# Queries and keys of three batches transposed by the DMA crossbar instead of TensorE, with a newly searched order of work

## The chip, the cores and the metric

The kernel runs on one core of a Trainium2 chip. The metric is the device time of one execution in microseconds (us). A single core has faster and slower executions too: one that is over 1.5% above the fastest of the same kernel is called slow, and ratios use fast runs alone.

A ratio below is the mean time of one kernel's fast runs over that of the kernel before in the same rounds, with a 95% interval. It is not quite the ratio of the medians that stand beside it. Where I turn a ratio into microseconds, I multiply its distance from 1 by 180 us.

## The reference

An attention over 4 batches, 8 heads, 768 positions and 64 dimensions feeds a gated long convolution. Each position sees 8 global keys and the last 96 positions.

```python
def _attn_ref(q, k, v, n_global, n_local):
    scores = scale * np.matmul(q, k.transpose(0, 1, 3, 2))
    # ... bias by distance, everything but global and local keys masked
    a = np.exp(scores - max)
    return np.matmul(a / sum, v)

def _moe_ref(x, w_proj, filter_fft, w_out):
    x1, x2, x3 = thirds of (x @ w_proj)
    x2_conv = irfft(rfft(x2) * rfft(filter_fft))
    return (x1 * x2_conv * x3) @ w_out
```

## The kernel before

The program is a graph of operations with costs. A list scheduler with searched weights (NUDGES) lays them out ahead of time, and each engine then runs its list in that fixed order. Loads of query, key and value rows are issued by GpSimd, stores and small copies by the SP queue.

Queries and keys arrive as rows and are needed with the head dimension on partitions. Batch 0 has its own path, which the change leaves alone. For batches 1 to 3, TensorE transposes four 128x128 blocks into a PSUM bank, and ScalarE or VectorE copies the bank out:

```python
self.qn = t("qn", [P, 6, H, D])      # rows, one buffer for all batches
self.kn = t("kn", [P, 7, H, D])
self.QT = t("QT", [P, 4, S])         # transposed, one buffer as well
self.KT = t("KT", [P, 4, 7 * P])

def transposes(self, what, t, src, cols):
    b = g.bank()
    def turn(_):
        for i in range(4):
            nc.tensor.transpose(b.f16()[:, P * i:P * i + P],
                                src[:, 2 * i:2 * i + 2, :], self.ident)
    g.op("P", pe(*[128] * 4), turn, acq=[b], ...)
    dst = ...                                    # a piece of QT or KT
    g.op("AV", ..., lambda e: self.copy(e, dst, b.f16()...), use=[b], ...)
    if what == "k" and t == 0:                   # the 8 global keys, to the front of each tile
        g.op("V", dve(224), lambda _: self.copy("V", kv[:, :, :, 0:NG], ...), ...)

def scores(self, hp, gi, near=False, pair=False):
    ...                                          # KT against QT, then exp on ScalarE
```

Because qn, kn, QT and KT exist once, they form a ring. A load of the next batch needs this batch's rows transposed, and a transpose needs the scores of the batch before to have read QT and KT.

The softmax here doesn't subtract the row's maximum and nothing guards it: scores larger than these inputs give would overflow.

Of the kernel before, what the change touches and what calls it, by code (L numbers as in the profile page):

```python
# [16 lines left out]
P = 128  # L17
NG = 8
# [21 lines left out]
BEGIN = 1.0  # L40
# [24 lines left out]
class Plan:  # L65
# [90 lines left out]
    def lay(self):  # L156
# [10 lines left out]
        out = []  # L167
        for o in self.ops:
            o.rank = o.batch[0] + o.batch[1] * o.tail / (total[o.batch] or 1.0) + o.bias + o.noise
        while live:  # L170
# [33 lines left out]
            if o.bytes:  # L204
                n, size = o.bytes
                cost = 0.007 + 3.6e-5 * size if e == "S" else 0.0045 + 3.7e-5 * size
                x = "SG".replace(e, "")
                at, work, each[e] = max(dma[e], o.end + 1.0), n * cost / 16, cost
                slow = 1.0 + each[x] / cost
                both = min(max(0.0, dma[x] - at), slow * work)  # L210
                dma[e] = at + both + work - both / slow
                ready = o.landed = dma[e] + 2.1
                if e == "G":
                    lanes.append(ready)
# [21 lines left out]
        -26671, 1454, -27060, 644, -34526, -2914, -25286, -6925, -45676, -4611, -20860, 1460, 2723, 7789,  # L236
        -8273, -9648, -2460, -18439, 5853, -13712, -13265, -5361, 9436, 3579, -30354, -6495, -3967, 2837,
        -13308, 7637, 1168, 7200, -12925, 8898, -12205, 12435, -32726, 4718, -4396, -6557, 7468, -1990,
        -3553, -11575, -8488, -6307, 8992, -12791, 23613, 4548, -30667, 7678, -2661, 40439, 23, 3822, 25223,
        19000, 9598, 7189, 9787, 23821, -11341, 23456, -11755, 5738, -6127, 39, 3279, 34899, -27473, 7686,  # L240
        5753, 21416, 6632, 26871, 8728, 6700, -3360, 18664, 10344, 10332, -16596, 12142, -10605, 14405,
        -25027, -150, 4813, -1741, 6716, 5345, -5698, 894, -21964, 8631, 14489, -201, 15618, 9598, 7510,
        4151, -7056, -21, 32636, 2899, -11225, -6462, 6929, -304, -21733, 21997, 9940, -5190, 9087, 636,
        -5187, -573, -12475, -4124, -8380, -671, -12776, 4813, -3686, 1361, -2133, 9833, -12744, 7014, 828,
        13335, 519, -7496, -1970, -5267, 3910, -7020, 8778, -5167, 3049, -39, 44238, -22392, 3868, -5492,
        5032, -11948, 883, -8512, 25357, -7798, 18676, -15531, 4417, -16339, 13865, -1852, 23684, -21598,
        13514, 17858, 17257, -557, 13373, 6339, 16373, -9272, -4058, -25687, 26062, 9023, 16287, -2105,
        6700, 2623, -3578, -5898, 15188, -9520, 15932, 4326, 21030, 6734, 2015, 1958, -25233, 9143, -34251,
        -13125, -16742, -592, -6891, -15887, -9801, -48606, -12178, 2086, -15877, -25133, -1600, 2379,
        -23801, -14531, 20195, 15173, 12449, 263, -17906, -3700, 14906, 1186, -19366, -14660, -2718, 3254,  # L250
        -20486, -7203, -4412, -15788, -38649, -6418, -1655, 10753, -17734, -21313, 32361, 393, 8516, -16517,
        21564, 1605, 17688, -3061, -10380, -4180, -14573, 4840, -13690, -17777, -9155, 18474, -7161, -29302,
        -313, -1665, -19374, -7420, -9795, 1024, -6732, 29494, 24754, -8266, -9187, -12630, 17723, 6915,
        -11585, 9057, -17244, -16606, 3040, -3366, 6885, -37386, 9683, -15183, -31661, -37889, -7819, 2466,
        -43791, -22140, 13121, -13710, 10401, 1807, 4765, 14336, -10814, -10169, 21045, -19960, 7933,
        -28620, 4211, -2811, 31233, 6868, -22348, 7890, -2864, -3743, 11427, -9576, 6080, -16630, 30799,
        1411, -4032, -3274, -9417, -2532, 9740, -10826, 28438, 5562, 26589, 793, -40417, 5892, -36342,
        -5644, 12849, -30590, 31141, 14444, -22328, -12896, -34168, -8150, -57913, -5204, 15711, 1235, 6293,
        2213, -6086, 8688, -22799, -4727, -21975, 17194, -3757, 10396, 28637, -4968, -17049, 3259, -12065,
        -270, -4906, -13608, 20080, -17815, 28876, 3572, -8777, -22175, -21175, 18592, 15224, -14329,  # L260
        -11261, -10500, -9164, -9393, 13199, -26402, -4645, -15202, -9299, -525, -6777, -7165, -9244, -9225,
        -12419, -15805, -7708, 2178, -7241, 5647, 21012, -4991, 6401, -2334, -5140, -15069, -20652, 5961,
        -35697, -3611, 3644, 12613, 47972, -1640, -2197, -11800, -5777, -7189, -2610, 3952, -203, 6913,
        15527, 7240, -16137, -6679, -3937, 834, -9611, 5105, 47, 4543, -11122, -4503, 13644, -16722, -24463,
        -17316, 12192, -10915, -20126, 1382, -8962, -10346, -24211, 12202, -33855, -21067, -21629, -2645,
        -5398, 11363, 4058, 2571, 6248, -2867, -3454, -7013, 8111, -4165, 25648, 9706, -4648, -11997, 8847,
        11920, -27944, -21197, 2222, -9255, -9101, -11207, -15647, 3068, 13863, -5612, 8378, 9103, -8882,
        -8677, -24972, -18852, -16277, -12182, 13199, -18976, -10170, 1364, 3773, 11230, 24038, 8526, 1626,
        15020, 3004, 30489, -4629, -331, 10528, 1419, 13574, 6549, 21821, 15228, 20766, 7684, 26770, 25798,
        -6498, -4789, -24449, -1245, -16178, 5655, -2810, 1595, 9574, 8409, 17611, 9924, -11306, 5323,  # L270
        12431, 4942, 33467, 24985, -10121, -311, -22495, 6019, -12210, 28768, -6886, -9465, 1431, 3236,
        14926, 8794, 2903, -275, -15940, 3474, 11924, 140, 18537, -2691, 3215, 4369, -7883, 10255, -2377,
        887, 1506, 8351, 2749, -2666, 1724, -2, -8763, -5759, 1279, 11205, -777, -15691, 3883, 5909, 4026,
        -9324, -6840, 3413, 6573, 10766, 6716, 11440, 1465, 3772, -14379, 1234, -13313, -5734, 7025, -2665,
        9733, -6834, 8271, 2042, 3032, -4621, 7425, -2600, 10085, -9127, 3381, -1345, 10211, -15378, 14859,
        6857, 8081, 211, -1467, -11827, -16185, 6723, -5950, -24265, -11782, -11476, -732, 5043, -7070,
        -927, -9965, 11218, -19986, 8589, -7968, 10143, 2808, 7080, -15962, 18025, -6488, -499, -21061,
        14160, 525, 514, -5066, -3068, 941, -12317, 489, 8578, 2311, -1959, -40040, 7983, 8312, 9946,
        -11449, 18822, -1699, 8498, 7623, 5090, -32147, 7079, 13071, 8675, -18625, 26688, 5401, 9760, -3054,
        -5688, 10887, 17782, -13291, 8915, -23867, 1484, -9206, 905, -50212, 11474, -9340, 12839, -13268,  # L280
        429, 3871, 17041, -25961, 10524, -8593, 29296, -26306, 6518, 14317, 1927, -27757, 14545, 15984,
        18775, -25044, -5453, 16461, 12339, -26421, 21502, 24783, 12969, -26891, 4376, 2513, 21873, 3194,
        -8112, -21024, 21259, -11197, 9391, -9675, -1356, 5710, -303, -16301, -11560, -30198, -10455, 6734,
        -10213, -20174, -19011, -27667, -4423, 4767, 13297, -32900, -12768, -27091, -7505, -2906, -20,
        34459, -2712, -3019, -702, -10293, -1211, 1634, 4234, -39114, -9749, 2253, 2533, 4712, 13540,
        -13115, -7066, 9629, 10055, 5131, 16930, -44240, -1286, 1203, 11673, -8416, 4726, -23705, 231,
        20816, 5391, -3140, 21876, 6812, 8588, -2283, 324, -40884, 10010, -9762, 8391, 14654, -15576, 1269,
        -1921, -1740, 998, -15686, -13359, -15492, -1021, 16161, -8349, -8154, 14786, -2046, 9528, -19999,
        1098, 10795, 12962, -13145, -12603, -1488, -5242, -44098, 21514, -2107, -9950, 17508, -780, -9857,
        6702, -3077, 14242, -28282, -6503, 2982, -12743, -9010, 2470, -6831, -13960, -21890, 6529, -21690,  # L290
        -992, -19558, -6249, -3225, 12323, -17611, -30223, 131, 4811, -10703, -2324, -2227, -11059, 5994,
        2855, -856, 5707, 21867, 785, 65, 15347, -11442, -3622, -17986, -7314, 12817, -2221, 2881, 9966,
        -2027, 698, 10775, -14082, -20635, 9561, -14262, 4552, -5388, 10443, -24604, -307, -2081, -2703,
# [89 lines left out]
        -8861, 21389, -11049, 17509, 41686, -10618, 9220, 25781, -14448, 18101, -8955, -3503, -7033, 43740,  # L383
        -10951, -8268, 11031, -2994, -4936,
    )
    FAVOUR = 0.1

    def fill(self, out):

# [75 lines left out]
class Fused:  # L465
# [173 lines left out]
    def load_v(self, b, ts):  # L639
# [4 lines left out]
        for t in ts:  # L644
            self.load_rows(("vn", s), vt, self.v, b, t)
            if t == 0:
                self.load_global(vt, s)
# [755 lines left out]
```

## Time and profile before

| | before |
|---|---|
| time, median (range) | 180.75 us (179.53 to 181.28, 4 runs of the comparison) |
| span of the profiled run | 179.1 us |
| TensorE busy | 170.3 us, 95% |
| VectorE busy | 161.0 us, 90% |
| ScalarE busy | 154.1 us, 86% |

The page below gives the DMA engines' busy share over 40 equal slices of the span (4.5 us each, 9 is 90% or more), the hardware queue (packets, MB, share of the time of 16 engines), and the row loads with their median time from issue to landing, the last number.

```profile
DMA  5999999999999999999990000000260000023344
...
q1 hardware_dynamic: 5920, 9.63, 15.1%
...
kn<-in_k_dram POOLq DMA_DIRECT2D x21, 120.0 KB, 6.2
qn<-in_q_dram POOLq DMA_DIRECT2D x18, 128.0 KB, 6.3
```

While loads run, up to about 93 us, the DMA row stands at 9 without a break. A digit adds up the time of all packets in the slice over 16 engines, and packets overlap: the queue of the row loads (q0, software_dynamic) alone has 107.1% of the span. So a 9 says that there are transfers in flight all the time, and no digit can show more.

### The profile page before, as it was taken

What the parts mean: (1) busy time and instruction counts of PE and PEld (TensorE: products, weight loads), DVE (VectorE), ACT (ScalarE), POOL (GpSimd) and SP (SyncE); (2) the same over time, 40 slices, a digit from 0 to 9 for tenths busy, and PEclk for the clock granted to TensorE, in tenths of its full rate; (3) what the DMA queues carried; (4) which work ended last, traced back from release to release, by engine and by line L of the source; (5) the groups of instructions that cost most, each with busy time, mean ns of one, the idle gap of its engine ahead of it and who ended that gap; (6) DMA issues with size and microseconds to landing.
All of it is one profiled execution on the core that took longest, in us unless ns stands there. A gap on an engine that the chain in (4) does not pass through costs nothing.

```text
span 179.1 us, 4509 instructions
## 1 busy us (share of the span) xinstructions
PE 170.3 (95%) x1732; PEld 105.3 (59%) x1732; DVE 161.0 (90%) x380; ACT 154.1 (86%) x311; POOL 70.0 (39%) x90
## 2 busy tenths in 40 slices
PE   7998799999999999999999999999999999999990
PEld 2456487566445657966456658854564784456540
DVE  6779679999999899999996998999999999999950
ACT  8699599987999999999869899999859997978751
POOL 7973692994988998998400000000000000000000
PEclk9999789999999999999999999999999999999997
DMA  5999999999999999999990000000260000023344
GB/s 184 334 251 112 167 207 166 149 177 140 182 150 140 120 146 114 129 158 139 170 298 21 0 4 0 4 0 0 103 243 10 4 2 0 4 115 119 117 176 178
DMA packets 79573, 21.19 MB, mean 118 GB/s; under 512 B 70424, under 2 KB 76480, under 8 KB 79552
## 3 DMA queue, kind: packets, MB, share of 16 engines
q0 software_dynamic: 73632, 11.28, 107.1%
q1 hardware_dynamic: 5920, 9.63, 15.1%
q8 instruction: 13, 0.21, 0.6%
q14 instruction: 8, 0.07, 0.1%
HBM read 25.69 MB, written 6.29 MB: 179 GB/s over the span
## 4 chain that ended last, share of the span: by engine, by line
PE 73%; DVE 8%; DMA 6%; POOL 4%; ACT 4%; issue 2%; POOLq 0%; ACTq 0%
PE bank L1085 22%; PE bank L1194 12%; PE bank L1146 9%; DMA vn<-in_v_dram 6%; PE bank L911 6%; PE bank L962 4%; PE bank L1168 4%; PE bank L925 4%; PE bank L1047 4%; PE bank L1002 4%; PE bank L1007 3%; POOL vn L575 2%; ACT E L977 2%; DVE E L984 1%; PE bank L1171 1%
## 5 line engine op out<-in xcount | busy, mean ns | idle before, releaser
L1085 PE MATMUL bank<-xT,w 128*128 128x384 f16 x256 | 44.4, 326 | 0.0
L977 ACT ACTIVATE E<-bank 128x864 f16<-128x864 f32 x48 | 40.6, 902 | 3.3 <-PE bank L962 3.3
L1085 PEld LDWEIGHTS <-w 128*128 128x128 f16 x256 | 24.4, 98 | 16.2 <-issue 0.6
L575 POOL DMA_DIRECT2D vn<-in_v_dram x28 | 25.9, 930 | 0.2 <-DVE E L689 0.2
L984 DVE TENSOR_TENSOR E<-E,mask 128x864 f16<-128x864 f16 x36 | 20.7, 596 | 1.9 <-ACT E L977 1.9
L1194 PE MATMUL bank<-wo,y 128*128 128x512 f16 x96 | 22.2, 379 | 0.0
L575 POOL DMA_DIRECT2D kn<-in_k_dram x21 | 19.3, 920 | 5.1 <-PE bank L925 2.1
L575 POOL DMA_DIRECT2D qn<-in_q_dram x18 | 16.3, 908 | 6.7 <-DMA g<-in_moe_filter_fft_dram 2.4
L563 ACT ACTIVATE ot<-bank 128x512 f32<-128x512 f32 x21 | 12.7, 612 | 7.0 <-PE bank L1194 6.5
L1002 PE MATMUL bank<-vn,E 128*128 128x65 f16 x224 | 16.3, 198 | 2.0 <-DMA vn<-in_v_dram 2.0
L1026 DVE TENSOR_TENSOR xn<-bank,rc 128x512 f16<-128x512 f32 (+1 forms) x23 | 17.2, 759 | 0.2
L1002 PEld LDWEIGHTS <-E 128*128 128x128 f16 x224 | 14.7, 100 | 4.4 <-DMA vn<-in_v_dram 2.5
L1095 ACT CAST g<-bank 128x384 f16<-128x384 f32 x32 | 15.7, 513 | 1.6 <-PE bank L1085 0.9
L563 ACT ACTIVATE ab<-bank 128x512 f16<-128x512 f32 x22 | 13.2, 623 | 3.7 <-PE bank L1146 3.7
L962 PE MATMUL bank<-QT,KT 64*128 64x216 f16 (+2 forms) x224 | 15.9, 244 | 0.3 <-DVE KT L559 0.3
L1007 PE MATMUL bank<-vn,E 128*128 128x65 f16 x192 | 16.1, 197 | 0.0
L563 ACT ACTIVATE x<-bank 128x384 f16<-128x384 f32 x28 | 13.9, 541 | 1.8 <-PE bank L1085 1.7
L1194 PEld LDWEIGHTS <-y 128*128 128x128 f16 x96 | 8.9, 98 | 10.3 <-issue 0.4
L1007 PEld LDWEIGHTS <-E 128*128 128x128 f16 x192 | 14.0, 100 | 0.5 <-issue 0.2
L559 ACT COPY QT<-bank 128x512 f16<-128x512 f16 (+1 forms) x19 | 11.7, 627 | 1.8 <-PE bank L617 1.5
L962 PEld LDWEIGHTS <-KT 64*128 64x128 f16 x224 | 8.4, 95 | 7.9 <-issue 5.3
L559 ACT CAST eo<-bank 128x384 f16<-128x384 f32 x28 | 12.2, 572 | 0.4 <-PE bank L1171 0.2
(147 smaller groups left out, 370.1 us busy)
## 6 DMA issues: line engine op xcount, KB each, us to landing
out_dram<-ot SPq DMA_DIRECT2D x24, 256.0 KB, 2.7
vn<-in_v_dram POOLq DMA_DIRECT2D x28, 120.0 KB, 6.7
kn<-in_k_dram POOLq DMA_DIRECT2D x21, 120.0 KB, 6.2
qn<-in_q_dram POOLq DMA_DIRECT2D x18, 128.0 KB, 6.3
ot<-in_q_dram SPq DMA_DIRECT2D x4, 384.0 KB, 3.1
h<-in_k_dram SPq DMA_DIRECT2D x4, 384.0 KB, 9.5
w<-in_moe_w_proj_dram POOLq DMA_DIRECT2D x4, 256.0 KB, 9.9
g<-in_moe_filter_fft_dram POOLq DMA_DIRECT2D x1, 768.0 KB, 11.0
```

The costliest lines, as they stand in the source:

```text
L559: {"A": nc.scalar.copy, "V": nc.vector.tensor_copy, "G": nc.gpsimd.tensor_copy}[e](out, in_)
L563: self.nc.scalar.mul(out, in_, c)
L575: return self.g.op(eng, 0.57 + 0.00035 * nbytes[0] if eng == "G" else 0.5, lambda _: e.dma_start(dst, src), w=w, r=r, nbytes=nbytes, name= ...
L962: nc.tensor.matmul(bs[hh].f32()[:, off:off + w], self.KT[hs, hp, P * m:P * m + P], self.QT[hs, hp, KL * m:KL * m + w], start=(off == 0 and ...
L977: g.op("A", act(864), lambda _: nc.scalar.activation(eo, bs[0].two()[:, :, 0:432].rearrange("p h (m w) -> p h m w", m=2), Act.Exp, scale=s ...
L984: g.op("V", dve(864, 2), lambda _: nc.vector.tensor_mul(eo, eo, mk), r=[("E", hp, gi), ("mask", hp)], w=[("E", hp, gi)], name="masked")
L1002: nc.tensor.matmul(o[:, n, hh], ef[:, at:at + P], vt[:, t, 2 * hp + hh, :], start=first, stop=(t == 0), skip_group_check=True)
L1007: nc.tensor.matmul(o[:, n, hh], ef[:, at:at + P], vt[:, t - 1, 2 * hp + hh, :], start=False, stop=True, skip_group_check=True)
L1026: nc.vector.tensor_mul(to, o[:, :, :, 0:D], rc.to_broadcast([P, 2, 2 * nt, D]))
L1085: nc.tensor.matmul(bk.f32()[:, 0:h], self.w[:, c, o + P * j:o + P * j + P], self.xT[:, c, h * s:h * s + h], start=(c == 0), stop=(c == 3))
L1146: nc.tensor.matmul(bk.f32(), src[:, c], w[:, c, DM:2 * DM], start=(c == 0), stop=(c == 3))
L1194: nc.tensor.matmul(bk.f32(), y[:, c, P * t:P * t + P], self.wo[:, c, :], start=(c == 0), stop=(c == 3))
```

## The change

The intent is to take the transposes and copies of batches 1 to 3 off TensorE, PSUM, ScalarE and VectorE and give them to the DMA engines. One transposing DMA replaces four TensorE transposes and a copy. The copies of the 8 global keys, which VectorE made after the transpose, are now made by DMA before it. The order of all work was searched again for the new costs.

```diff
+    CROSS = (1, 2, 3)
...
+    def cross(self, what, t, src, cols):
+        dst = (self.QT if what == "q" else self.KT)[:, :, cols:cols + P]
+        keys = [("kng", min(t // 2, 1))] if what == "k" else []
+        self.g.op("S", 1.2, lambda _: self.nc.sync.dma_start_transpose(
+            out=dst, in_=src.rearrange("p h d -> p (h d)")), r=[(what + "n", t)] + keys,
+            w=[(what.upper() + "T", t)], nbytes=(128, 1800), name=what + "T")
...
+                turn = self.cross if b in self.CROSS else self.transposes
                 for t in new:
-                    self.transposes("q", t, self.qn[:, t], P * t)
+                    turn("q", t, self.qn[:, t], P * t)
                 for t in self.GRP[c]:
-                    self.transposes("k", t, self.kn[:, t], P * t)
+                    turn("k", t, self.kn[:, t], P * t)
...
+                if t == 0 and b in self.CROSS:
+                    self.load_global(self.kn, ("kng",), ("kn", 0))
```

Cut here: all of NUDGES (new values), FAVOUR from 0.1 to -0.1, the scheduler's cost of an SP transfer, a shorter gap before the first filling matmuls, and load_global made general.

## The prediction

> **What bounds the kernel now.** I read the page from the top: busy shares, then the slices, then the chain that ended last, then the groups, and last the stretches and the waits that the trace answers for.
>
> The page's first part gives the engines' busy time; its fourth the chain that set the end.
>
> ```profile
> span 179.1 us, 4509 instructions
> ...
> PE 170.3 (95%) x1732; PEld 105.3 (59%) x1732; DVE 161.0 (90%) x380; ACT 154.1 (86%) x311; POOL 70.0 (39%) x90
> ...
> PE 73%; DVE 8%; DMA 6%; POOL 4%; ACT 4%; issue 2%; POOLq 0%; ACTq 0%
> ```
>
> The tensor engine is on 73% of the chain, but VectorE (90%) and ScalarE (86%) are close behind, so a change that helps TensorE alone could be stopped by the other two. Because a matmul's end is modelled, 170.3 us is not pure work. The rate at which matmuls follow each other is seen in the chain in order of time (start, length, what):
>
> ```profile
> 101.86 0.45 PE bank L925 x8
> 102.30 0.29 PE bank L962 x6
> 102.60 5.31 PE bank L1085 x32
> 107.90 0.48 PE bank L962 x12
> 108.39 0.33 PE bank L925 x4
> ...
> 113.14 0.89 PE bank L925 x16
> ```
>
> The reader is to see that these pieces touch: in the middle of the kernel TensorE goes from one to the next without a gap, and a transpose of 128 columns (line 925) takes 0.89/16 = 0.056 us. With such rates from the same view (0.166 for line 1085, 0.216 for the 512-column ones, 0.03 for lines 1002 and 1007, 0.04 for line 962) I sum the groups: about 42 + 52 + 14 + 10 + 11 + 6 + 9 + 14 for small groups and fill = some 158 us of matmul in 179. Of the other 21 us some 10 are the start and the end; the rest are short bubbles.
>
> The groups that the change removes (line, engine, operation; count; busy us, mean ns):
>
> ```profile
> L925 PE MATMUL bank<-ident,kn 128*128 128x128 f16 x84 | 7.3, 219 | 0.3 <-DMA vn<-in_v_dram 0.3
> L925 PE MATMUL bank<-ident,qn 128*128 128x128 f16 x72 | 6.5, 220 | 0.0
> L559 ACT COPY QT<-bank 128x512 f16<-128x512 f16 x17 | 10.1, 606 | 0.3
> L559 ACT COPY KT<-bank 128x480 f16<-128x480 f16 x14 | 8.0, 594 | 0.0
> L559 DVE COPY KT<-bank 128x480 f16<-128x480 f16 x7 | 2.8, 399 | 0.1
> ```
>
> 156 transposes and 38 copies out of PSUM stand here (one query copy more fell to VectorE), nearly all the copies on ScalarE.
>
> Which stretch they lie in (us; busy of PE, PEld, DVE, ACT, POOL; clock; DMA; GB/s):
>
> ```profile
> 21.00:35.00 14.00, 13.81 (x206) 9.87 (x205) 12.72 (x38) 12.00 (x22) 9.77 (x12) 0.91 1.83 178
> 35.00:60.00 25.00, 24.36 (x247) 14.81 (x245) 24.10 (x62) 23.05 (x44) 20.63 (x23) 1.00 2.22 157
> 60.00:90.00 30.00, 29.94 (x310) 18.81 (x307) 29.55 (x62) 28.21 (x56) 25.39 (x29) 1.00 2.63 141
> 90.00:118.00 28.00, 28.00 (x331) 19.03 (x330) 25.46 (x54) 24.97 (x48) 0.00 (x0) 1.00 0.19 47
> ```
>
> All of line 925 lies between 35.5 and 115.4 us, where TensorE is full, VectorE about 95% full and ScalarE 91%. Loads run until about 93 us and then stop, so in this kernel the inputs of batch 3 are there more than 20 us before their last use. The first 21 us belong to batch 0, which the change leaves as it is: the chain there is one 11.55 us wait for the first value rows.
>
> **What the Trainium skill says.** "VectorE: DVE Perf Modes", section "The three transpose paths", gives 390 ns for a 128x128 transpose on TensorE and 1309 ns by the DMA crossbar, the first ending in PSUM and the second in SBUF. The trace agrees on the kind but not the cost of the first: alone it shows 219 ns, and in a row 56 ns, which is what it costs the chain here. "TensorE: Matmul & The Clock Gate", section "Wait — 56ns, not 53.3ns?", gives that same 55 to 56 ns warm; the trace agrees. "DMA: Bandwidth & Descriptors", section "Anatomy of one DMA — SWDGE (gpsimd) path", puts a fixed part of about 2 us on a transfer, so a transposing transfer will never be as quick as the TensorE path; here the output stores, from the other path, land 2.7 us after issue and the loads 6.2 to 6.7. No run of before shows a crossbar transpose. The same page, "Issuing engines are not separate DMA queues", says all queues share 16 engines: the trace, with loads landing in 4.7 to 11.9 us, fits, though it does not isolate it.
>
> **The change, part by part.**
> 1. *TensorE.* Three batches times (6 query + 7 key) tiles = 39 tiles of 4 transposes: 156 x 0.056 = **8.7 us** off a stretch where TensorE has no gaps. The weight loads go with them.
> 2. *Copies.* ScalarE loses 10.1 + 8.0 = 18.1 us. VectorE loses 2.8, one query copy (0.42) and three 224-column copies of the global keys (some 1.3 with waits on its port, the longest 0.51): about **4.5 us**. In the stretch 21 to 118 us, VectorE goes from 91.8 to 87.3 us busy and ScalarE from 88.2 to 70.1. If the stretch shrinks by 9 to 88 us, VectorE would be 99% busy, too full, so the new order must hand ScalarE some copies that VectorE does now. There is enough: the PSUM copies that may go to either (xT 6.1, X 4.1, eo 2.2, x1 2.2, ot 2.0, ab 1.4 us) are 18 us on VectorE; 6 to 8 of them bring VectorE to about 80 and ScalarE to about 78. This is a choice of the search that I take for granted.
> 3. *PSUM.* 39 bank uses go, each a matmul group of 0.22 us and a copy of 0.4 to 0.6 us: less waiting for a free bank. I count 1 us for it, an estimate without a row.
> 4. *Added DMA.* 39 transposing transfers of 128 KB and 6 small copies of global key rows (like the vn<-vn copies, 0.69 us of issue each), all on the SP queue. From the skill's 1309 ns for a quarter of such a tile, I estimate 1.2 to 2 us of issue and 3 to 6 us to landing. 39 x 1.5 = 60 us of SP work over 85 us: SP computes nothing, so it fits beside other work. On the data engines: 67 row loads need about 0.92 us of issue each, 62 us in all, in the 85 us that they take; 13 transposes per batch at some 0.6 us of all engines (an estimate from 128 KB at about 200 GB/s, as the loads move) are 8 us per batch, 25 in all. The loads will be spread over more time, perhaps to 105 or 115 us; the 20 us of lead in before pays for that.
> 5. *Order and warm-up.* Fewer filling matmuls before the first transpose. The first stretch ends with the landing of value rows at 19 to 20 us, so I give it 0 to 0.5 us.
>
> Sum: 8.7 + 1 + 0.3 off, 0.5 to 1 for new waits on: 180.35 - 9.5 = **170.8 us**. A check by shares: matmul time falls by 8.7/158 = 5.5%, the two copying engines' work by 22.6/315 = 7.2%; scaled by 5.5%, the time would be 170.4.
>
> **The rivals.**
> (a) *A DMA wait replaces the TensorE work.* The single buffers for queries, keys and their transposes make a ring: a transpose waits for the scores of the batch before, a load waits for the transpose. The GpSimd queue already waits for line 925 (4.4 us in five waits), and each link gets 2 to 5 us longer. SP takes its queue in order, and the waits of the SP queue show output stores that hold it:
>
> ```profile
> SPq L1202 <- ACT ot L563: 88.0, 19, 36.0
> SPq L575 <- DMA vn<-in_v_dram: 62.6, 3, 32.8
> ```
>
> A transpose behind a late store is late as well. Against: attention of one batch is interleaved with the convolution of the one before, so TensorE has other work. Each of three batches could lose 2 to 3 us: 176 to 179 us.
> (b) *VectorE becomes the bound.* If the copies are not handed over, VectorE's 156 us and its present 18 us of idle time give 174 to 175.
> (c) *Bubbles vanish too.* With ScalarE at 76% the exponentials come sooner and 3 to 4 us more of the 11 us of bubbles go: 166 to 167.
> (d) *The data engines slow down.* If a transpose holds all of them for 2 us, 78 us of the loading time are gone and loads come late for batches 2 and 3: 180 or above. The mean of 140 to 160 GB/s against 334 in the second slice speaks against so full a system.
>
> **Range and chances.** Main path 60%, around 169 to 173; (c) 15%; (b) 12%; (a) 10%; (d) 3%. That makes 166 to 176 the range for 8 in 10. Faster by over 2% means below 176.7: the main path, (b), (c) and a part of (a), 0.88; within 2% 0.09; slower 0.03.
>
> **What would show it.** Right: no transposing matmul is left in batches 1 to 3, TensorE's instructions fall from 1732 to about 1570, ScalarE's busy time to 140 to 145 us, VectorE's to 148 to 155, TensorE's to about 161, its idle time stays near 9 us, and the last load is issued between 95 and 120 us. The scores (line 962) wait for no transpose for more than 2 us in total. Wrong: waits of line 962 on DMA of the transposed tiles of 3 us or more (a); VectorE at 93% or more of the span (b); loads landing in 10 us and values (line 1002) waiting for them (d). The step I trust least is the time to landing of a transpose, which no row of before measures.

## The result, and the profile after

The kernel after took 201.95 us (median, 200.19 to 204.71, 4 runs) against 180.75. The ratio of the fast runs is 1.1099 (1.0993 to 1.1205): **slower by 11%**. The profiled run is a fast one. First its page: span, busy times, and the share of each engine in the chain that ended last.

```profile
span 198.8 us, 4251 instructions
...
PE 167.5 (84%) x1574; PEld 97.0 (49%) x1574; DVE 153.1 (77%) x363; ACT 143.0 (72%) x282; POOL 71.7 (36%) x90
...
PE 45%; DMA 44%; POOL 4%; DVE 2%; issue 2%; ACT 0%; SPq 0%; POOLq 0%
```

The work left TensorE, ScalarE and VectorE as planned, but DMA went from 6% of the chain to 44%. The lines that answer to those of before, from the same page:

```profile
DMA  5999999999999999999999999950004300004245
...
q1 hardware_dynamic: 27352, 14.92, 39.6%
...
kn<-in_k_dram POOLq DMA_DIRECT2D x21, 120.0 KB, 11.4
qn<-in_q_dram POOLq DMA_DIRECT2D x18, 128.0 KB, 12.1
```

A slice is now 5.0 us, so the row stands at 9 to about 129 us instead of 93. A row load takes almost twice as long to land. The list of DMA issues gives the transposes, with their median time to landing (of those whose landing the trace knows, about half):

```profile
KT<-kn SPq DMA_TRANSPOSE x21, 8.6
QT<-qn SPq DMA_TRANSPOSE x18, 8.1
```

Four query transposes of batch 3, issued from 120.5 us on, after the last load had been issued at 111.6, show what one takes with next to nothing beside it (duration of the issue on SP as min/median/max ns and first and last start, then landing in us):

```profile
L938 SPq DMA_TRANSPOSE QT<-qn x4: 1219/1224/1404, 120.5 to 130.6; - x4
...
DMA to landing us min/median/max: 2.4/2.4/2.4
```

The landing is known for one of the four, and a key transpose at 132.0 us has the same. The same operation thus lands in 2.4 us alone and in some 8 beside loads. What it does to the scores (line 966) is in the waits (us in total, times, longest):

```profile
ACT E L981 <- PE bank L966: 26.4, 10, 8.4
PEld L966 <- DMA KT<-kn: 22.0, 5, 8.7
PE bank L966 <- DMA KT<-kn: 20.0, 5, 8.3
...
PE bank L966 <- DMA QT<-qn: 3.0, 2, 1.5
```

TensorE stands still 20.0 + 3.0 = 23.0 us for transposed tiles, and ScalarE's exponentials behind it for 26.4. The chain in order of time (start, length, what) shows where:

```profile
34.81 9.31 DMA kn<-in_k_dram
...
44.41 8.41 DMA vn<-in_v_dram
52.82 11.15 DMA KT<-kn
...
91.83 9.86 DMA QT<-qn
```

From 34.81 us on, the end of the program hangs on loads and then on a transpose of keys: batch 1. At 91.83 us it hangs on a transpose of queries once more. The value load in this chain is a doubtful name. The trace has the rows of the transpose at 52.82 us landed at 44.12. What stood before it was SP's fixed order: the key transpose ahead of it was issued at 51.28 us, as soon as a key load of 39.84 us had landed (51.26). The stretches show the hole (PE, PEld, VectorE, ScalarE, GpSimd, granted clock of TensorE, DMA share as in the DMA row but without its limit, GB/s):

```profile
35.00:60.00 25.00, 15.91 (x86) 6.48 (x84) 16.55 (x43) 11.76 (x22) 16.27 (x18) 0.86 2.09 138
60.00:90.00 30.00, 17.60 (x215) 10.52 (x215) 18.79 (x42) 16.23 (x27) 16.25 (x18) 0.87 1.98 141
90.00:118.00 28.00, 25.37 (x182) 13.52 (x181) 21.33 (x43) 21.83 (x46) 14.75 (x16) 0.90 2.56 134
```

Before, TensorE had 24.36, 29.94 and 28.00 us of work in these stretches: 23.4 us more, which is about the time that was lost. GpSimd was busy 20.63 and 25.39 us in the first two and done by 90 us; now it works into the third. The lower granted clock goes with the stops: the kernel without transposes that e5 below runs has 1.00 in all three.

Neither the DMA share nor the GB/s rise in the first two stretches: 2.09 and 1.98 where before has 2.22 and 2.63, and 138 and 141 GB/s where before has 157 and 141. What the transposes do to the loads shows in the landings, and in the waits of GpSimd's queue: by name, its row loads wait 21.7 us in all for earlier row loads (1.9 us in e5), and none waits for a transpose. Each of these waits in after is for the load eight before: the query load of 68.84 us was issued 0.3 us after that of 50.64 us had landed (68.55). So a late landing also makes a later load late.

### The profile page after: what moved, and what is told of

It is laid out like the page before. It is cut to its first block, busy times and chain, and to the rows that moved or that the text cites. A ratio compares the mean times of both kernels' runs of the same rounds, so it can differ in the third digit from the quotient of the medians.

```text
span 198.8 us, 4251 instructions
## 1 busy us (share of the span) xinstructions
PE 167.5 (84%) x1574; PEld 97.0 (49%) x1574; DVE 153.1 (77%) x363; ACT 143.0 (72%) x282; POOL 71.7 (36%) x90
## 2 busy tenths in 40 slices
DMA packets 101004, 26.46 MB, mean 133 GB/s; under 512 B 91688, under 2 KB 97912, under 8 KB 100984
## 3 DMA queue, kind: packets, MB, share of 16 engines
q1 hardware_dynamic: 27352, 14.92, 39.6%
## 4 chain that ended last, share of the span: by engine, by line
PE 45%; DMA 44%; POOL 4%; DVE 2%; issue 2%; ACT 0%; SPq 0%; POOLq 0%
DMA vn<-in_v_dram 20%; PE bank L1089 13%; PE bank L1199 8%; PE bank L1151 7%; DMA g<-in_moe_filter_fft_dram 7%; DMA QT<-qn 7%; DMA KT<-kn 6%; DMA kn<-in_k_dram 5%; PE bank L966 3%; PE bank L1173 3%; PE bank L906 3%; PE bank L1006 2%; POOL vn L571 2%; PE bank L1011 2%; PE bank L1051 1%
## 5 line engine op out<-in xcount | busy, mean ns | idle before, releaser
L981 ACT ACTIVATE E<-bank 128x864 f16<-128x864 f32 x48 | 40.7, 892 | 26.7 <-PE bank L966 26.4
L1089 PE MATMUL bank<-xT,w 128*128 128x384 f16 x256 | 48.3, 333 | 0.0
L966 PE MATMUL bank<-QT,KT 64*128 64x216 f16 (+2 forms) x224 | 18.3, 260 | 23.0 <-DMA KT<-kn 20.0
L571 POOL DMA_DIRECT2D vn<-in_v_dram x28 | 26.8, 962 | 14.8 <-DMA vn<-in_v_dram 3.9
L1089 PEld LDWEIGHTS <-w 128*128 128x128 f16 x256 | 24.0, 99 | 16.4 <-issue 2.0
L1101 DVE TENSOR_TENSOR g<-g,x 128x384 f16<-128x384 f16 x32 | 10.9, 349 | 10.9 <-ACT x L559 8.4
L559 ACT ACTIVATE x<-bank 128x384 f16<-128x384 f32 x30 | 15.0, 500 | 5.9 <-PE bank L1089 3.2
L559 ACT ACTIVATE ot<-bank 128x512 f32<-128x512 f32 x24 | 14.2, 606 | 5.7 <-PE bank L1199 5.6
L1099 ACT CAST g<-bank 128x384 f16<-128x384 f32 x32 | 15.1, 492 | 3.0 <-PE bank L1089 2.3
L559 ACT ACTIVATE ab<-bank 128x512 f16<-128x512 f32 x21 | 12.4, 610 | 6.0 <-PE bank L1151 5.8
L1006 PE MATMUL bank<-vn,E 128*128 128x65 f16 x224 | 16.4, 197 | 0.0
L1011 PEld LDWEIGHTS <-E 128*128 128x128 f16 x192 | 13.6, 99 | 0.8
L555 ACT CAST X<-bank 128x512 f16<-128x512 f32 x21 | 11.8, 604 | 2.2 <-PE bank L906 2.2
## 6 DMA issues: line engine op xcount, KB each, us to landing
kn<-in_k_dram POOLq DMA_DIRECT2D x21, 120.0 KB, 11.4
qn<-in_q_dram POOLq DMA_DIRECT2D x18, 128.0 KB, 12.1
```

What stands on the lines that cost most here:

```text
L559: self.nc.scalar.mul(out, in_, c)
L571: return self.g.op(eng, 0.57 + 0.00035 * nbytes[0] if eng == "G" else 0.5, lambda _: e.dma_start(dst, src), w=w, r=r, nbytes=nbytes, name= ...
L966: nc.tensor.matmul(bs[hh].f32()[:, off:off + w], self.KT[hs, hp, P * m:P * m + P], self.QT[hs, hp, KL * m:KL * m + w], start=(off == 0 and ...
L981: g.op("A", act(864), lambda _: nc.scalar.activation(eo, bs[0].two()[:, :, 0:432].rearrange("p h (m w) -> p h m w", m=2), Act.Exp, scale=s ...
L1006: nc.tensor.matmul(o[:, n, hh], ef[:, at:at + P], vt[:, t, 2 * hp + hh, :], start=first, stop=(t == 0), skip_group_check=True)
L1011: nc.tensor.matmul(o[:, n, hh], ef[:, at:at + P], vt[:, t - 1, 2 * hp + hh, :], start=False, stop=True, skip_group_check=True)
```

## The experiments

My theory after reading the trace: the transposes and the row loads slow each other on the DMA engines, and the scores wait for what comes late. The rivals were the new order (bad by itself), the number of small packets, a lack of lead for the transposes (lead is the time from the arrival of the rows to the first use of the transposed tile), and a removal worth less than I thought. All but one of the 18 runs passed the comparison with the reference. That says little here: kernels whose scores miss the transposes passed it as well, since scores are small beside the bias.

### The new order with the transposes on TensorE (e1_order_pe)

The edit in words, since the code is long:

```diff
-  crossbar transpose at its place in the searched order
+  four TensorE transposes and a ScalarE copy at that place,
+  or at the next one where a PSUM bank is free
```

> The changed kernel's order of work, but each of the 39 crossbar transposes is put back on TensorE (four transposes and one ScalarE copy out of PSUM, at the same place in the order; the global key rows still come by DMA). Contention theory (the crossbar transposes share the 16 data engines with the row loads, which had them nearly full already): the time comes back to 176 to 186 us, the row loads land in 6 to 7 us again instead of 10 to 12, and the scores wait for no DMA. Order theory (the new search found a bad order): it stays at 195 us or above.

Measured: 202.67 us, ratio 1.1313 (1.1207 to 1.1419). The row loads land in 5.6 to 6.6 us again, so without transposes on the queue the loads are quick in this order too. But ScalarE waited 12.5 + 11.2 us for the inserted TensorE transposes. The run puts work of two busy engines at places chosen for an idle queue, and so can't tell the theories apart. e5 below shows that the order is sound.

### Fewer packets in the loads (e2_wide_after, e3_wide_before)

Rows of queries and keys are read as whole 2 KB pieces (wrong rows), so that such a load has 120 to 128 packets and not 960 to 1024. Value loads keep theirs.

```diff
-        src = self.q[b, :, P * t:P * t + P, :].rearrange("h p d -> p h d")
+        src = self.q[b].rearrange("h (a c) d -> (h a) (c d)", c=8)[P * t:P * t + P]
```

> Wrong result on purpose: in the changed kernel the query and key rows of batches 1 to 3 are read as contiguous rows of 2 KB, so a load of the same bytes has 120 to 128 packets in place of 960 to 1024 (the value rows stay as they are). Contention theory, in packets: the load phase ends before 100 us, the transposes land in 3 to 6 us instead of 8 to 9, the scores wait less than 8 us for them, and the time is 165 to 180 us. Order theory or a fixed cost of a transpose: still 193 us or above with landings of 8 us.

> The partner of the run before: the kernel before with the same wide reads (wrong result on purpose). It has no transposes on the data engines. Contention theory: little to gain, 175 to 181 us, since loads were hidden; and the changed kernel with wide reads is faster than this one by 3 to 6 per cent, as the blind sum had it. If the wide reads alone make this kernel as much faster as the changed one, the wide pair says nothing of the transposes.

Measured: e2 202.26 and 200.87 us in its two fast runs (205.54 median with two slow ones, no ratio). All packets together fall from 101,004 to 66,060, but transposes land in 9.5 to 9.7 us, key and query loads in 8.9 and 11.2, and TensorE waits 22.4 us for keys. The packet count of these loads is not the cause. e3, the same in the kernel before: 179.47 us, ratio 0.9992 (0.99 to 1.0083), no difference.

### Transposes added to the kernel before (e4_ghost, e4b_ghost)

The kernel before keeps its TensorE transposes, and each tile is transposed by the crossbar as well, into a target that nobody reads as scores (the edit of e4b, its target shortened).

```diff
                 nc.tensor.transpose(b.f16()[:, P * i:P * i + P],
                                     src[:, 2 * i:2 * i + 2, :], self.ident)
+            nc.sync.dma_start_transpose(out=ghost, in_=src.rearrange("p h d -> p (h d)"))
```

> The kernel before as it is, plus 39 crossbar transposes of the same tiles at the same times into memory that nobody reads (TensorE still does the real ones). Contention theory: the row loads land in 9 to 12 us instead of 6 to 7, the loading phase goes on to 110 us or later, and the time rises to 184 to 200 us though nothing waits for the transposes themselves. Latency theory (only the scores' wait for a late transpose costs): within 2 per cent of before.

> The first such run with its fault mended (the extra transpose was put after the next load of its source tile): the kernel before, in which TensorE still does every transpose, with 39 extra crossbar transposes of the same tiles into memory that nobody reads, issued beside the TensorE ones. Contention theory: loads land in 9 to 12 us instead of 6 to 7, loading lasts to 110 us or more, 184 us or above. Waiting theory (only scores that wait for a late transpose cost): within 2 per cent of before.

Measured: e4 234.69 us, ratio 1.3045. It was faulty: the added transposes came after the next load into the same rows. e4b, mended: 219.56 us, ratio 1.2243 (1.21 to 1.2386). Here no score waits for a crossbar transpose, and yet the kernel loses 22%. TensorE waits 10.2 us for key rows and 10.0 for query rows. But the key and query loads do not as a rule land late, as I had expected (9 to 12 us): their medians are 6.9 and 7.3 us, though single ones take up to 14.0. They are issued late, and GpSimd waits up to 11.7 us before one. My reading, argued and not shown, is that an SP queue that runs late holds the rows. The targets made waits of their own (ScalarE 10.3 us), so I take only this from it: added transposes can cost through the issue of the loads, with no score waiting for them.

### The same order with the transposes left out (e5_none_after)

```diff
-        self.g.op("S", 1.2, lambda _: self.nc.sync.dma_start_transpose(
-            out=dst, in_=src.rearrange("p h d -> p (h d)")), r=[...
+        self.g.op("S", 1.2, lambda _: None, r=[...
```

> The changed kernel with its 39 crossbar transposes simply left out (the scores of batches 1 to 3 then use the tiles of batch 0: wrong on purpose; all other work, loads and global copies stay). This is its order of work with transposes that cost nothing. Transpose theory (landing 8 to 9 us where the order left 0 to 3 us of slack, and loads slowed from 6 to 11 us): 165 to 175 us. Order theory (the new order is bad by itself, as the run with TensorE transposes put into it, 202.7 us, would have it): 190 us or above. In between, the difference to 202 is the transposes' part and the rest the order's.

Measured: 175.35 us, ratio 0.9785 (0.9709 to 0.9861). The key and query loads land in 6.5 and 7.3 us. Its page:

```profile
span 171.7 us, 4147 instructions
...
PE 160.6 (94%) x1574; PEld 94.4 (55%) x1574; DVE 153.4 (89%) x363; ACT 141.9 (83%) x282; POOL 70.6 (41%) x90
```

This kernel is after with transposes that cost nothing. From it to after is 1.1099 - 0.9785 = 0.1314, or 23.7 us, against 23.0 us of waits for transposed tiles in the profile. The two are not quite the same sum: between the profiled runs (e5's is its fastest) lie 27.1 us, of which TensorE is idle 20.2 us longer and takes 6.9 us more for the same 1574 instructions, at the lower clock. So the order isn't at fault. It also says that a perfect crossbar would have gained 0.0215 x 180 = 3.9 us (2.5 to 5.2) in this order and not 9.5.

### The kernel before with its transposes left out (e6_none_before, e12_none_before_shift)

e6 leaves out the TensorE transposes and copies of batches 1 to 3 and moves nothing. e12 also gives 12 PSUM copies of VectorE to ScalarE at the same places.

```diff
             for i in range(4):
-                nc.tensor.transpose(...)
+                pass
...
-        g.op("AV", ..., lambda e: self.copy(e, dst, ...), use=[b],
+        g.op("AV", ..., lambda e: None, use=[b],
... e12 alone, in the finished order:
+            if o.eng == "V" and o.name in ("X", "eo", "ab", "x1") and 25.0 < o.start < 112.0:
+                o.eng = "A"
```

> The kernel before with the 156 TensorE transposes of batches 1 to 3, their 39 copies and the three copies of global keys left out, nothing put in their place (wrong on purpose), order as it is. It is the most that could be had in the old order: the blind sum says 8.7 us plus 1, so 169 to 172 us. If TensorE is not what bounds this kernel, it is 176 us or above.

> The kernel before with the transposes of batches 1 to 3 and their copies left out (as in the run that had 175.8 us, wrong on purpose), and besides 12 copies out of PSUM that VectorE did between 35 and 120 us given to ScalarE (some 7.6 us by the rows of before). If VectorE is what kept that run from the 170 us of the blind sum: 171 to 174 us. If the fixed order and its waits kept it: 175 us or above.

Measured: e6 175.79 us, ratio 0.9831 (0.9768 to 0.9894), which is 3.0 us. TensorE's busy time falls by 8.0 us to 162.3, but its idle time in the span grows from 8.8 to 13.6 (in the profiled run, 177.72 us, the slowest of the five). In the stretch where VectorE was fullest (columns as above):

```profile
60.00:90.00 30.00, 27.45 (x258) 15.84 (x257) 28.97 (x61) 22.57 (x42) 25.16 (x28) 1.00 2.77 151
```

VectorE is busy 28.97 us of 30, TensorE no longer all of it. That suggested VectorE as the new bound, and e12 was to test it: 176.67 us, ratio 0.9901 (0.9829 to 0.9974). VectorE fell from 156.6 to 153.0 us in all, and nothing was gained; in this stretch it still has 28.65. By what I had written down, that speaks for the fixed order and its waits. But the fullest stretch stayed full, so VectorE as the bound is neither confirmed nor excluded. Why the removal gives 3 to 4 us and not 9.5 stays open.

### Plain copies in place of transposes (e7_copy_after)

Same place, bytes and tiles, but an ordinary copy of 128 KB within SBUF (wrong; the edit is shortened).

```diff
-        self.nc.sync.dma_start_transpose(out=dst, in_=src.rearrange("p h d -> p (h d)"))
+        self.nc.sync.dma_start(dst, src.rearrange("p (i a) d -> p i (a d)", i=4))
```

> The changed kernel with each crossbar transpose replaced by a plain copy of the same 128 KB from the same tile to the same place by the same queue (wrong on purpose). If any transfer of that size beside the loads does it: 195 us or above with landings of 7 us or more. If it is the crossbar's own: landings of 3 to 5 us and 174 to 182 us. I hold the first for somewhat likelier (0.6).

Measured: 191.78 us, ratio 1.0696 (1.0583 to 1.0809). From its list of DMA issues:

```profile
KT<-kn SPq DMA_DIRECT2D x21, 128.0 KB, 8.0
...
QT<-qn SPq DMA_DIRECT2D x18, 128.0 KB, 6.8
```

Landings came as in the first of my two cases, the time between both. A plain copy lands almost as late as a transpose (2.3 us at its best), and TensorE waits 13.3 us for keys. Its issue takes 0.65 us on SP, a transpose's about 1.2. In ratios: 0.9785 with nothing, 1.0696 with copies, 1.1099 with transposes. Of the 23.7 us, 0.0911 x 180 = 16.4 us come with any such transfer at that place and 7.3 us more with the crossbar. Crossbar and copy differ in landing and in issue at once, so I can't say which of the two makes the 7.3.

### The transposes with most loads left out (e11_noload_after)

After, with nearly all query and key loads of batches 1 to 3 and the value loads of batches 2 and 3 left out (output wrong). The edit is shown for the queries.

```diff
         self.load("G", self.qn[:, t], src, [("qn", t)], (1024, 256), f"q{t}")
+        self.g.ops[-1].fn = lambda _: None
```

> The changed kernel without most of the row loads of batches 1 to 3 (queries and keys, and the values of batches 2 and 3, are not loaded: wrong on purpose), all 39 crossbar transposes kept, order kept. Contention theory: with the loads gone the transposes land in 2.4 to 3.5 us, the scores wait under 3 us for them, and the time is that of the run without transposes or less, 168 to 177 us. If a crossbar transpose is slow by itself, landings stay at 8 us and the time above 190.

Measured: 180.08 us, ratio 1.0033 (0.9922 to 1.0145). The DMA issues:

```profile
KT<-kn SPq DMA_TRANSPOSE x21, 2.8
QT<-qn SPq DMA_TRANSPOSE x18, 3.4
```

The same 39 transposes land in 2.8 and 3.4 us, and no score waits for one. The run also holds the contrast within itself. The last row load that is left is issued at 39.6 us and lands in 8.6. Query transposes issued from 21.8 to 43.5 us land in 8.1 to 12.5 us; those issued from 55.0 us on land in 2.5 to 3.9. So for the landings this is the other half of the proof: in this order loads are quick without transposes (e5), transposes are quick without loads (here), and together both are slow.

The time missed what I had expected (168 to 177 us). Another load, that of the filter, came late and made VectorE wait 9.2 us (2.6 in e5). That this makes the 4.5 us between the two ratios is argued, not shown.

### The old order with the crossbar in some batches (e8, e9, e10 and their repeats)

In the finished order of before, the TensorE transposes and copies of chosen batches are dropped, and each crossbar transpose is inserted on SP as soon as its rows are there and its target is free (by a function recross, left out here). This separates the batches: batch 3 has the most lead, batch 1 none.

```diff
+    CROSS = (3,)          # e8;  (2, 3) in e10;  (1, 2, 3) in e9
-        return self.program(self.fill(self.lay()))
+        return self.program(self.fill(self.recross(self.lay())))
```

Several of these had faults of mine. In e9, 10 of the 39 transposes came after the next load of the same rows. In e8, e8b, e10 and e13 the copy of a batch's global keys stood before TensorE transposes of the batch before, which then waited for it.

> The order of the kernel before, but the transposes of batch 3 alone go through the crossbar, each issued as soon as the plan has its tile loaded and its target free (6 to 30 us ahead of its first use in the plan). The loads end at about 93 us, so most of these transposes run beside no loads. Transpose theory: landings of 2.4 us for those after the loads, no wait of the scores, a third of the gain of the run with nothing in place: 175 to 179 us. If a crossbar transpose costs the kernel something apart from loads and lead, it is 180 or above.

> A repeat of the run with batch 3 alone through the crossbar, of which three of four executions were in the slow state. 177 to 181 us, within 2 per cent of before; a gain above 2 per cent would be against the run with nothing in place of the transposes, which gained 1.7 per cent.

> The order of the kernel before with all 39 transposes through the crossbar, issued as early as the plan allows (7 to 30 us ahead of first use, where the changed kernel's plan often has 5 to 8). Slack theory (only the missing lead of the new order costs): landings of 8 us are hidden, 170 to 177 us. Contention theory (loads slowed for all, so batch 1 arrives late whatever the order): 183 to 200 us, with loads landing in 9 to 12 us and waits of the first scores of batch 1 for the transposes.

> The run before this one with its fault mended (10 of the 39 transposes came after the load of the next batch into the same tile and so waited up to 54 us for it): the order of the kernel before, all 39 transposes through the crossbar, each as early as the plan has its tile loaded and its target free. Slack theory (the new order only gave too little lead): 172 to 178 us, no score waits over 2 us in total. Contention theory (transposes and loads slow each other for as long as both run): 183 to 198 us, transposes landing in 7 to 10 us, loads in 9 to 12.

> Order of the kernel before, batch 1 transposed on TensorE as there, batches 2 and 3 through the crossbar as early as the plan allows. In the run with all three batches the one long stall was 18.2 us, for a transposed query tile of batch 1, and that run was 18 to 20 us slower than before. Theory: batch 1 has no lead, because its rows arrive just in time, and a crossbar transpose beside the loads needs 8 us to land and 1.8 us of queue; batches 2 and 3 have lead. Then this run is 177 to 183 us with no score wait above 3 us. If instead the crossbar costs through the loads in every batch: 190 us or more.

> A try at a version that beats both: batches 2 and 3 through the crossbar in the old order, and the same 12 copies moved from VectorE to ScalarE. If VectorE binds and the crossbar of batches 2 and 3 is hidden: 174 to 178 us. Else as the run without the shift, 178 to 183 us.

Measured:

- Batch 3 alone: e8 178.14 us in its one fast run (181.41 median, no ratio); e8b 180.08, ratio 1.0057 (1.0002 to 1.0112), with 3.0 us of the wait that I had made (read from a slow run, the one that was profiled).
- Batches 2 and 3: e10 190.65, ratio 1.0648, of which my fault is a wait of 7.4 us. That is the dearer of the two cases. GpSimd held a key load of batch 3 for 12.4 us until batch 2's keys were transposed, and the four query and key loads that it issued after 100 us landed in 14.9 to 16.8 us. e13, the same with copies moved as in e12: 189.93, ratio 1.0619, inside e10's interval, where I had hoped for 183 at most.
- All three: e9 211.77 (faulty, 1.1836); e9b, mended, 200.41 (fast runs 199.05 and 197.8, no ratio). Its transposes land in 6.8 and 8.0 us, but its query and key loads in 6.5 and 6.9, not in the 9 to 12 that I had expected. These medians hide the place that counts: the five query and key loads issued from 32 to 46 us, before the wait below, land in 10.0 to 16.6 us, where before has 6.3 to 9.3.

In e9b one wait stands out, with its echo on the load queue:

```profile
POOL qn L616 <- DMA QT<-qn: 25.9, 3, 13.0
...
PE bank L1017 <- DMA QT<-qn: 18.2, 1, 18.2
```

It is the first use of batch 1. Four key and three query transposes take SP 13.4 us of issue there, 1.8 and 2.1 us each against 1.2 alone. Why an issue is longer there is not shown (in e11 single ones take 2.0 to 2.3 us after the last row load has landed, too). So the old order with early transposes loses about as much as the searched one. The cause lies in the transfers, not in the search.

The last two runs mend the place of the global copies.

> The order of before with only batch 3's queries and keys turned by the crossbar, as in e8 and e8b, but with batch 3's copy of its global keys put after the last TensorE turn of batch 2 (in e8b those turns waited 3.0 us for that copy). Theory (a crossbar turn is cheap where it has lead and no loads beside it): 177 to 180 us, the 3.0 us gone and a third of the about 3 us that the removal is worth gained, ratio 0.985 to 1.0. Rival (turns by DMA cost time even there): 181 us or more, ratio above 1.005, with waits of scores for turned tiles.

> The order of before with batches 2 and 3 turned by the crossbar, batch 1 on TensorE; the copies of global keys of batches 2 and 3 put after the last TensorE turn of batch 1 (in e10 those turns waited 7.4 us for batch 2's copy). Theory (only batch 1, whose rows arrive with no lead, pays for the crossbar): 177 to 184 us, ratio 0.985 to 1.02. Rival (turns beside loads cost in every batch): 188 us or more, ratio above 1.04, with landings of 6 us or more for the keys of batch 2 and a later load of batch 3.

```diff
+                before |= {x for x in out if getattr(x, "kturn", None) == o.cross[3] - 1}
```

Measured: **e8c 178.11 us, ratio 0.9895 (0.9844 to 0.9947)**: faster than before by 1%, and so than after. The gain is small: the plain mean of its five fast runs, over that of the five fast runs of before in the same comparison, is 0.993. The step from e8b, 0.0162 or 2.9 us, fits my 3.0 us of wait. Of its 13 transposes all but the first are issued from 89.3 us on, when GpSimd has issued its last load, and no score waits for one. The first, at 82.2 us beside loads, landed in 7.3 us. Its stretch from 90 us (columns as above):

```profile
90.00:118.00 28.00, 27.93 (x302) 17.61 (x300) 25.62 (x53) 20.77 (x40) 0.00 (x0) 1.00 0.59 115
```

TensorE stays full, and ScalarE has 20.77 us of work where it had 24.97.

e10b missed my expectation: 189.53 us (two fast runs of six, 187.85 and 186.33), ratio 1.0455 (1.0369 to 1.054). I had said that only batch 1 pays; the rival came true. Batch 2 pays as well, 1.0455 - 0.9895 = 0.056 or 10 us, although its rows are there earlier. Its profiled run fell in a slow state (granted clock 0.661), so I read no times from it. It shows the same kind of wait as e10's fast one, a load of batch 3 held by a transpose of batch 2. That this makes the 10 us is argued, not shown.

## Why the prediction was wrong

The direction was wrong, and 201.95 lies far outside 166 to 176. Step by step:

**The step that failed** is the fourth, "SP computes nothing, so it fits beside other work" and "the 20 us of lead in before pays for that", with "0.5 to 1 for new waits on" in the sum. That term measured 23.7 us (e5 to after; 23.0 in the waits). Three things were wrong inside it.
- The landing. I gave "3 to 6 us". It is 2.4 alone, but 8.1 and 8.6 in the place where it was used.
- The loads. I had them spread out by 25 us of data-engine time. They were slowed down themselves, from 6.2 and 6.3 us to 11.4 and 12.1. I had written the Trainium skill's statement that all queues share 16 engines ("DMA: Bandwidth & Descriptors", section "Issuing engines are not separate DMA queues") beside it, and the DMA row of nines was on the page. I set it aside for the GB/s, 140 to 160 against a peak of 334, as proof of room. In after they are 138 and 141, with landings twice as long: bytes per second did not tell whether there was room.
- The lead. The 20 us that I counted lie in batch 3, and run to the last use of its rows and not to the first. The transposes of batch 1 follow rows that come just in time, and there the chain hangs on them.

**The value of the removal**, "8.7 + 1 + 0.3 off", was mis-sized too: 3.0 us in the old order (e6), 3.9 in the new (e5). The count was right, TensorE has 8.0 us less work in e6, but its idle time grew. Rival (b), VectorE as the bound at 174 to 175 us, gave the size of e5 and e6 (175.35 and 175.79); its mark, VectorE at 93% of the span, did not appear (89%), and e12 did not confirm it.

**The rivals.** (a) and (d) happened together. (a) had the right mark, scores waiting for transposed tiles 3 us or more, but I made it 2 to 3 us a batch, against 23.0 in all. (d) had the right mark as well, loads landing in 10 us, and was given 3%. Counted as exclusive, each looked small; in after late loads make late transposes (the key rows that land at 51.26 us) and late loads as well. The way back that (a) named, a transpose that holds the rows for the next load, is not in the waits of after, where loads wait for loads. It is there in other runs: GpSimd waits for transposed tiles 26.8 us in e2, 25.9 in e9b and 12.4 in e10.

**Smaller slips of reading.** The 219 ns that I called a transpose alone are the mean length of one record within a row of four. The three copies of global keys take VectorE 0.9 us, not 1.3. The 2 us of fixed time stand in a section on GpSimd's path, while the transposes go by SP; the 2.4 us that they took alone happen to be near it. None of this enters the sum.

**What was right.** TensorE's instructions (1574, predicted about 1570), ScalarE's 143.0 us (140 to 145), VectorE's 153.1 (148 to 155), with copies handed to ScalarE as assumed, and the last load issued at 111.6 us (95 to 120). TensorE's busy time came out at 167.5 instead of 161, though 160.6 in e5, and its idle time at 198.8 - 167.5 = 31.3 instead of 9. These counts say what moved, not what it costs.

**What stays open.** How transposes or copies and loads slow each other on the engines; it is not the packets of the query and key loads. Why the removal gives no more than 3 to 4 us. What exactly batch 2 loses in e10b.

## What to carry to other kernels

Work given to a queue that computes nothing was free here only where its transfers had a free place: use the DMA row of the slices to see where other transfers are in flight, don't take the GB/s for room, and take the landing time from the stretch where the transfer will run. A single-buffered ring of load, transpose and use can turn a late landing into a late load (e2, e9b, e10). Move the part that has lead and no loads beside it (here batch 3, 1%), and first run the kernel with the work simply left out, since that bounds the gain (for that order; here 2%, before any cost).

## What the Trainium skill lacked or had wrong

- "VectorE: DVE Perf Modes", "The three transpose paths", gives one figure for the crossbar, 1309 ns for 128x128. The runs show that a figure alone is not enough: four such blocks in one transfer of 128 KB need 1.2 us of issue and land in 2.4 us alone, but in 8.1 to 8.6 us beside row loads.
- "Advanced Engine Details and Errata", "X-Bar Transpose (TRN2)", says that transposing DMAs are as fast as regular ones. At their best they land alike (2.4 us, a plain copy 2.3), but the issue on SP takes 1.2 us against 0.65, and the kernel with transposes is 7.3 us slower than with copies.
- "DMA: Bandwidth & Descriptors", "Rules for kernel authors", says that a transpose next to ordinary DMAs needs nothing. The comparison here is too insensitive to say anything of the data. As to time the page is silent: query loads go from 6.3 to 12.1 us in after, and transposes land in 2.4 us alone, in 8.1 to 8.6 beside loads.
- That the transfers of all queues share the engines stands in the skill, as said above. What it can cost stands on no page: key and query loads from GpSimd's queue land in 11.4 and 12.1 us in after against 6.5 and 7.3 without the transposes (e5), and key and query transposes from SP in 8.6 and 8.1 us against 2.8 and 3.4 with most loads left out (e11), at 138 and 141 GB/s in after.
